# Routing early, and two experts begun on the rows of the first six sequences

## The chip, the cores and the metric

The kernel runs on one core of a Trainium2 chip. A time is the device time of one execution, in microseconds (us). The engines are called by these names: PE (TensorE, matmuls), DVE (VectorE), ACT (ScalarE), POOL (GpSimd, which also issues transfers) and SP (SyncE, which only issues transfers).

## The reference

Two stages are computed, one after the other.

```python
# attention: 8 sequences, 8 heads, 576 positions, head size 64; causal in blocks of 64
scores = scale * q @ k.T
scores = where(pos_i // 64 >= pos_j // 64, scores, -1e9)
attn_out = softmax(scores) @ v
x = attn_out.transpose(0, 2, 1, 3).reshape(4608, 512)

# experts: a hash of the token id chooses one of 8 experts for each of the 4608 rows
expert_idx = token_ids * 2654435761 % 8
for e in range(8):
    rows = expert_idx == e
    out[rows] = maximum(x[rows] @ w1[e], 0) @ w2[e]      # w1: 512 x 1024, w2: 1024 x 512
```

The multiplier is odd and leaves 1 when divided by 8, so the expert of a token is the low three bits of its id. In the data used here the experts have between 525 and 624 tokens each, and between 402 and 471 of each expert's tokens are in the first six sequences.

## The kernel before

**Attention.** The work is cut into 32 pairs of heads, four pairs for each of eight sequences, and a loop of 34 rounds (g) goes over them as a pipeline. Round g computes the scores and exponentials of pair g (`S_chunk`, three chunks, line 289 on ACT), the product with v of pair g-2 (`PV`, lines 326 and 331), its division by the row sums (`norm`, lines 343 and 346 on DVE), and the transposes of q and k for pair g+2 (`T_pair`, lines 231 and 236). The casts of q and k to bf16 are made on DVE (line 171), with a last part on POOL (line 176), those of v on POOL (`cast_v`, lines 183 to 188), three rounds ahead. The loads of q, k and v of a sequence are issued by SP (lines 105 to 132) into the pool `ld`, which has two buffers of each, so the loads of sequence b+2 wait until the casts of sequence b have been made. A finished sequence is written as 576 rows to `x_dram` by POOL (`write_x`, lines 356 and 358).

**Routing.** While attention runs, a generator `route` works out a slot for every token: each expert owns 640 slots, that is five tiles of 128 (CAP and G), and 32 spare tiles take what overflows. It counts tokens with a scan along each partition and two small matmuls, and turns the counts into slot numbers with some twenty DVE instructions (lines 373 to 448). In rounds 2 to 8 one piece of it is run in each round. Then `place_a` and `place_b` turn the slots of one sequence into a permutation: DVE builds one-hot matrices (lines 490 and 493), POOL multiplies them with row numbers (496 and 499), PE multiplies the two (509) and DVE adds the result up (512). They run in rounds 11 to 26, in turn; `placed` in round 27 writes the permutation `perm3`.

**Experts.** For every expert, `gather_x` fetches five tiles of rows of x by an indirect transfer from POOL (line 633) into ten fixed buffers, `transpose_x` transposes them on PE (645) and copies them out on DVE (646), `stage_a` multiplies with w1 (64 matmuls of 320 columns, line 657) and applies the relu on ACT (662), and `stage_b` multiplies with w2 (40 matmuls of 512 columns, line 672), copies out on DVE (677) and scatters the rows to the output from POOL (679). The order on PE is: first layer of expert e, transposes of expert e+1, second layer of expert e-1. The weights have two buffers each and are loaded by POOL (531 and 536).

The order of instructions on each engine is that in which the program writes them (`manual_schedule`). Buffers of pools that follow one another in time lie over each other: those of the expert stage take the room of the attention pools, `fix` first, then `ld`. A pool's tile waits for the readers of what lay there before.

What joins the two stages is the following. Each gather of expert 0 names the whole of `x_dram` as its source:

```python
out=xgs[g % (2 * G)][:], out_offset=None, in_=x_dram[:, :],
in_offset=bass.IndirectOffsetOnAxis(ap=perm3[:, g : g + 1], axis=0),
```

so it waits for the rows of all eight sequences.

Of the kernel before, what the change touches and what calls it, by code (L numbers as in the profile page):

```python
# [22 lines left out]
N = B * S  # L23
NT = 4
NP = H // 2
CAP = 640
G = CAP // 128
OVT = 32
NG = E * G + OVT
NEG = -30000.0  # L30
# [4 lines left out]
def kernel(  # L35
# [50 lines left out]
    psS = att_ctx.enter_context(tc.tile_pool(name="psS", bufs=2, space=bass.MemoryType.PSUM))  # L86
    psT = att_ctx.enter_context(tc.tile_pool(name="psT", bufs=2, space=bass.MemoryType.PSUM))
    psO = att_ctx.enter_context(tc.tile_pool(name="psO", bufs=1, space=bass.MemoryType.PSUM))
    fix = att_ctx.enter_context(tc.tile_pool(name="fix", bufs=1))
    ld = att_ctx.enter_context(tc.tile_pool(name="ld", bufs=2))  # L90
    att = att_ctx.enter_context(tc.tile_pool(name="att", bufs=2))
    rt = att_ctx.enter_context(tc.tile_pool(name="rt", bufs=1))

# [276 lines left out]
    def route():  # L370
# [8 lines left out]
        for i in range(5):  # L379
# [19 lines left out]
        ohf = oh[:].rearrange("p e t -> p (e t)")  # L399
        nc.vector.tensor_tensor_scan(cum[:].rearrange("p e t -> p (e t)"), ohf, ohf, 0.0,  # L400
                                     op0=ALU.add, op1=ALU.bypass)
        offs = rt.tile([P, E], F32, name="offs")
        nc.vector.memset(offs[:, 0:1], 0.0)
        nc.vector.tensor_copy(offs[:, 1:E], cum[:, 0 : E - 1, T - 1])
        cnt = rt.tile([P, E], BF16, name="cnt")
        nc.vector.tensor_tensor(out=cnt[:], in0=cum[:, :, T - 1], in1=offs[:], op=ALU.subtract)
        pb = psT.tile([P, 5, 65], F32, name="pb", tag="tp")
        nc.tensor.matmul(pb[:, 0, 0:E], lhsT=lower[:], rhs=cnt[:], start=True, stop=True)
        nc.tensor.matmul(pb[:, 1, 0:E], lhsT=onesbf[:], rhs=cnt[:], start=True, stop=True)
        base = rt.tile([P, 2, E], F32, name="base")  # L410
        nc.vector.tensor_copy(base[:], pb[:, 0:2, 0:E])
        yield

        ovc = rt.tile([P, E], I32, name="ovc")
        nc.vector.tensor_scalar(ovc[:], base[:, 1, :], float(127 - CAP), 0.0, op0=ALU.add, op1=ALU.max)
        nc.vector.tensor_single_scalar(ovc[:], ovc[:], 7, op=ALU.arith_shift_right)
        ovf = rt.tile([P, E], F32, name="ovf")
        nc.vector.tensor_copy(ovf[:], ovc[:])
        inc = rt.tile([P, E], F32, name="inc")
        nc.vector.tensor_tensor_scan(inc[:], ovf[:], ovf[:], 0.0, op0=ALU.add, op1=ALU.bypass)  # L420
        e640 = rt.tile([P, E], F32, name="e640")
        nc.vector.tensor_single_scalar(e640[:], iota_e[:], float(CAP), op=ALU.mult)

        off1 = rt.tile([P, E], F32, name="off1")
        nc.vector.tensor_tensor(out=off1[:], in0=base[:, 0, :], in1=offs[:], op=ALU.subtract)
        off2 = rt.tile([P, E], F32, name="off2")
        nc.vector.tensor_tensor(out=off2[:], in0=inc[:], in1=ovf[:], op=ALU.subtract)
        nc.vector.tensor_scalar(off2[:], off2[:], 128.0, float(E * CAP - CAP), op0=ALU.mult, op1=ALU.add)
        nc.vector.tensor_tensor(out=off2[:], in0=off2[:], in1=e640[:], op=ALU.subtract)
        nc.vector.tensor_tensor(out=cum[:], in0=cum[:], in1=off1[:, :, None].to_broadcast([P, E, T]), op=ALU.add)  # L430
        ovm = rt.tile([P, E, T], F32, name="ovm")
        nc.vector.tensor_single_scalar(ovm[:], cum[:], float(CAP) + 0.5, op=ALU.is_gt)
        nc.vector.tensor_tensor(out=ovm[:], in0=ovm[:], in1=off2[:, :, None].to_broadcast([P, E, T]), op=ALU.mult)
        nc.vector.tensor_tensor(out=cum[:], in0=cum[:], in1=ovm[:], op=ALU.add)
        nc.vector.tensor_tensor(out=cum[:], in0=cum[:], in1=e640[:, :, None].to_broadcast([P, E, T]), op=ALU.add)
        nc.vector.scalar_tensor_tensor(out=cum[:], in0=cum[:], scalar=-1.0, in1=oh[:],
                                       op0=ALU.add, op1=ALU.mult)
        yield
        slf = rt.tile([P, T], F32, name="slf")
        nc.vector.tensor_reduce(slf[:], cum[:].rearrange("p e t -> p t e"), axis=AX.X, op=ALU.add)  # L440
# [93 lines left out]
    def load_w2(e):  # L534
        w2b = wts.tile([P, FF // P, DM], BF16, name="w2b", tag="w2b")
        nc.gpsimd.dma_start(w2b[:], moe_w2[e].rearrange("(p fb) o -> p fb o", p=P))
        w2s[e] = w2b


    NPAIRS = B * NP  # L540
    both = (nc.sync, nc.scalar)
    load_qk(0, 0, 2, rest=False, engs=both)
    load_qk(0, main=False, engs=both)
    load_qk(0, 2, 8, rest=False, engs=both)
    load_v(0)
    nc.sync.dma_start(tid[:], moe_token_ids.rearrange("(b s) -> b s", b=B))
    load_qk(1)
    load_v(1)
    rgen = route()
# [3 lines left out]
    for w in range(2):  # L553
        cast_qk(0, w, 0, 0)
    T_rest(0)
    for w in range(2):
        cast_qk(0, w, 1, 2, rest=False)

    steps = {g: (lambda: next(rgen, None)) for g in range(2, 9)}
    steps[7] = rows  # L560
    for j in range(B):
        steps[11 + 2 * j] = lambda j=j: place_a(j)
        steps[12 + 2 * j] = lambda j=j: place_b(j)
    steps[27] = placed
    for g in range(NPAIRS + 2):
        b, pr = divmod(g, NP)
        live = g < NPAIRS
        nxt = live and b + 1 < B
        if live:
            S_chunk(g, 0)  # L570
        if g >= 2:
            PV(g - 2, 0)
        if live:
            S_chunk(g, 1)
        if g >= 2:
            PV(g - 2, 1)
            norm(g - 2)
        if live:
            S_chunk(g, 2)
            if pr == 0:  # L580
                S_rest(b)
        if g == 0:
            T_pair(1)
        if g < 2:
            for w in range(2):
                cast_qk(0, w, g + 2, g + 3, rest=False)
        if g + 2 < NPAIRS:
            T_pair(g + 2)
        for gv in range(NP) if g == 0 else (g + 3,):
            bv, pv = divmod(gv, NP)  # L590
            if bv < B:
                cast_v(bv, pv)
                if pv == 0:
                    cast_v4(bv)
        if g in steps:
            steps[g]()
        if nxt:
            if pr == 0:
                cast_qk(b + 1, 0, 0, 2)
            elif pr == 1:  # L600
                cast_qk(b + 1, 1, 0, 2)
            elif pr == 2:
                T_rest(b + 1)
                cast_qk(b + 1, 0, 2, 4, rest=False)
            else:
                cast_qk(b + 1, 1, 2, 4, rest=False)
        if pr == 1 and b >= 1:
            write_x(b - 1)
        if pr == (1 if b == 0 else 0) and b + 2 < B:
            load_qk(b + 2)  # L610
            load_v(b + 2)
        if 6 <= g < 6 + 2 * G:
            nc.gpsimd.memset(xgs[g - 6][:], 0.0)
        if pr == 0 and b == 6:
            load_w1(0)
        if pr == 0 and b == 7:
            load_w2(0)
    att_ctx.close()


# [6 lines left out]
    HC = CAP // 2  # L627
    xtiles = {}

    def gather_x(e):  # L630
        for t in range(G):
            g = e * G + t
            nc.gpsimd.indirect_dma_start(  # L633
                out=xgs[g % (2 * G)][:], out_offset=None, in_=x_dram[:, :],
                in_offset=bass.IndirectOffsetOnAxis(ap=perm3[:, g : g + 1], axis=0),
                bounds_check=N - 1, oob_is_err=False,
            )

    def transpose_x(e):
        xT = mx.tile([P, NKT, CAP], BF16, name="xT", tag="xT")  # L640
        for t in range(G):
            xg = xgs[(e * G + t) % (2 * G)]
            tp = psX.tile([P, NKT, P], BF16, name="tpx", tag="tpx")
            for db in range(NKT):
                nc.tensor.transpose(out=tp[:, db, :], in_=xg[:, db * P : (db + 1) * P], identity=identbf[:])  # L645
            nc.vector.tensor_copy(xT[:, :, t * P : (t + 1) * P], tp[:])  # L646
        xtiles[e] = xT

    def stage_a(e):
        w1b = w1s[e]  # L650
        xT = xtiles[e]
        hT = mx.tile([P, NFT, CAP], BF16, name="hT", tag="hT")
        for ft in range(NFT):
            hp = psH.tile([P, 2, 512], F32, name="hp", tag="hp")
            for db in range(NKT):
                for t in range(2):
                    nc.tensor.matmul(  # L657
                        hp[:, t, 0:HC], lhsT=w1b[:, db, ft::NFT],
                        rhs=xT[:, db, t * HC : (t + 1) * HC],
                        start=(db == 0), stop=(db == NKT - 1),  # L660
                    )
            nc.scalar.activation(hT[:, ft, :].rearrange("p (t n) -> p t n", t=2), hp[:, :, 0:HC], ACT.Relu)  # L662
        return hT

    out_writes = []

    def stage_b(e, hT):
        w2b = w2s[e]
        for tt in range(G):
            yp = psY.tile([P, DM], F32, name="yp", tag="yp")  # L670
            for ft in range(NFT):
# [14 lines left out]
                tc.declare_no_dep(ins.ins, w.ins, reason="rows of different tokens")  # L686
            out_writes.append(ins)

    gather_x(0)
    gather_x(1)  # L690
    load_w1(1)
    load_w2(1)
    hts = {}
    transpose_x(0)
    for e in range(E):
        hts[e] = stage_a(e)
        if e + 2 < E:
            load_w1(e + 2)
        if e + 1 < E:
            transpose_x(e + 1)  # L700
        if e + 2 < E:
            gather_x(e + 2)
        if e >= 1:
            stage_b(e - 1, hts.pop(e - 1))
            if e + 1 < E:
                load_w2(e + 1)
    stage_b(E - 1, hts.pop(E - 1))


    n_ov = nc.values_load(ov_i[0:1, 0:1], min_val=0, max_val=OVT)  # L710
# [68 lines left out]
```

The softmax here doesn't subtract the row's maximum and nothing guards it: scores larger than these inputs give would overflow.

## Time and profile before

| quantity | value |
|---|---|
| time, median of 3 runs (lowest to highest) | 345.86 us (343.06 to 347.33) |
| span of the profiled run | 343.6 us |
| PE, DVE, ACT, POOL busy | 277.1, 158.8, 142.8, 198.1 us |
| mean granted clock of PE | 0.926 |
| last norm of attention ends | 162.45 us |
| first matmul with w1 begins | 179.87 us |
| second layer of expert 0 begins | 204.67 us |

The page of the profile gives the busy time of each engine, then 40 slices of the span in which a digit is the busy share in tenths; PEclk is the clock that PE was granted, and the DMA line is the share of the core's 16 DMA engines. The timeline lists an engine's instructions in order, with start, duration, engine, line, operation, result and operands, count, and in brackets the idle time before it and what ended that. The list of waits gives engine and line, whom it waited for, the sum in us, how often and the longest.

### The profile page before, as it was taken

The numbers are of one execution on the slowest core, as the hardware profiler recorded it, in microseconds if no ns is written. First come the engines' busy times: TensorE is split into PE (matmuls) and PEld (weight loads), VectorE is DVE, ScalarE is ACT, GpSimd is POOL, SyncE is SP. The second block draws the span as 40 slices with busy tenths as digits, with TensorE's granted clock in tenths as the row PEclk, the third lists the DMA queues.
The fourth block names the chain that finished last, engine by engine and source line by source line (L and its number), as shares of the span: only waits on it lengthen the run. The fifth ranks groups of instructions, "written<-read, shape, count | busy, mean of one in ns | idle before, by whom it ended". The sixth has DMA issues, their size and how long they took to land. (4 is left out here: it accounts for less than half of the span.)

```text
span 343.6 us, 7894 instructions
## 1 busy us (share of the span) xinstructions
PE 277.1 (81%) x3247; PEld 201.2 (59%) x3247; DVE 158.8 (46%) x346; ACT 142.8 (42%) x169; POOL 198.1 (58%) x281
## 2 busy tenths in 40 slices
PE   1574784998878888895039989999999999999991
PEld 1342663776656666664028865949586685949540
DVE  4345769888868788863020224040413324040330
ACT  1342762887657577783004440604133140604100
POOL 3065378388988789960374647274664737232352
PEclk9997886999989899997558999999999999999998
DMA  7999997899898984672226987796969697825432
GB/s 200 284 272 283 246 273 173 216 280 268 211 288 184 285 184 78 138 134 72 69 85 126 215 194 240 167 215 176 200 203 186 231 175 225 194 77 134 129 130 75
DMA packets 67045, 64.58 MB, mean 188 GB/s; under 512 B 19378, under 2 KB 60340, under 8 KB 64960
## 3 DMA queue, kind: packets, MB, share of 16 engines
q0 software_dynamic: 12288, 35.71, 43.5%
q1 hardware_dynamic: 52064, 27.17, 32.4%
q10 hardware_dynamic: 2656, 1.18, 1.3%
q8 instruction: 26, 0.43, 0.5%
q14 instruction: 11, 0.09, 0.1%
HBM read 67.15 MB, written 15.20 MB: 240 GB/s over the span
## 5 line engine op out<-in xcount | busy, mean ns | idle before, releaser
L289 ACT ACTIVATE pt<-ps 128x1024 bf16<-128x1024 f32 x96 | 94.3, 1022 | 54.3 <-PE ps L265 54.0
L662 ACT ACTIVATE hT<-hp 128x640 bf16<-128x640 f32 x64 | 45.0, 703 | 117.1 <-PE hp L657 117.1
L657 PE MATMUL hp<-xT,w1b 128*128 128x320 bf16 x512 | 72.7, 303 | 0.6 <-DVE xT L646 0.6
L657 PEld LDWEIGHTS <-w1b 128*128 128x128 bf16 x512 | 69.9, 144 | 3.2 <-issue 1.1
L672 PE MATMUL yp<-w2b,hT 128*128 128x512 bf16 x320 | 70.2, 379 | 0.0
L679 POOL DMA_INDIRECT out_dram<-ysb,perm x40 | 39.7, 992 | 35.6 <-DVE ysb L677 26.8
L646 DVE COPY xT<-tpx 128x512 bf16<-128x512 bf16 x40 | 15.7, 422 | 79.4 <-PE tpx L645 77.4
L672 PEld LDWEIGHTS <-hT 128*128 128x128 bf16 x320 | 31.0, 98 | 36.2
L677 DVE COPY ysb<-yp 128x512 f32<-128x512 f32 x40 | 27.7, 692 | 51.7 <-PE yp L672 51.7
L633 POOL DMA_INDIRECT xg<-x_dram,perm x40 | 40.6, 1015 | 16.5 <-issue 11.9
L326 PE MATMUL O<-vx,pt 128*128 128x65 bf16 x896 | 43.7, 206 | 2.6 <-DVE xs L346 2.2
L243 PE MATMUL ps<-qkT 64*128 64x64 bf16 (+2 forms) x384 | 37.9, 280 | 2.6 <-ACT pt L289 2.2
L326 PEld LDWEIGHTS <-pt 128*128 128x128 bf16 x896 | 35.8, 105 | 6.4 <-issue 1.8
L183 POOL CAST vx<-vf 128x512 bf16<-128x512 f32 x32 | 21.1, 669 | 20.9 <-DMA vf<-in_v_dram 19.9
L645 PE MATMUL tpx<-identbf,xg 128*128 128x128 bf16 x160 | 15.0, 229 | 19.9 <-DMA xg<-x_dram,perm 16.7
L356 POOL DMA_DIRECT2D x_dram<-xs x32 | 23.3, 734 | 13.1 <-DVE xs L346 12.6
L346 DVE TENSOR_TENSOR xs<-O,rs 128x320 bf16<-128x320 f32 x64 | 28.4, 486 | 1.1
L265 PE MATMUL ps<-maskq,maskk 64*128 64x64 bf16 (+1 forms) x256 | 28.3, 214 | 0.0
L645 PEld LDWEIGHTS <-xg 128*128 128x128 bf16 x160 | 11.0, 101 | 23.7 <-DMA xg<-x_dram,perm 18.0
L236 DVE COPY qkT<-tp 128x1024 bf16<-128x1024 bf16 x32 | 22.0, 688 | 5.0 <-PE tp L231 4.0
L531 POOL DMA_DIRECT2D w1b<-in_moe_w_dram x8 | 4.9, 614 | 30.8 <-PE tpx L645 26.7
L231 PE MATMUL tp<-identbf,qb 128*128 128x128 bf16 x128 | 13.7, 233 | 8.2 <-DVE qb L171 8.0
(112 smaller groups left out, 264.3 us busy)
## 6 DMA issues: line engine op xcount, KB each, us to landing
vf<-in_v_dram SPq DMA_DIRECT2D x16, 512.0 KB, 7.1
w1b<-in_moe_w_dram POOLq DMA_DIRECT2D x8, 1024.0 KB, 8.1
w2b<-in_moe_w_dram POOLq DMA_DIRECT2D x8, 1024.0 KB, 8.6
qf<-in_q_dram SPq DMA_DIRECT2D x7, 1024.0 KB, 7.9
kf<-in_k_dram SPq DMA_DIRECT2D x14, 512.0 KB, 7.1
x_dram<-xs POOLq DMA_DIRECT2D x32, 128.0 KB, 5.8
qf<-in_q_dram SPq DMA_DIRECT2D x16, 64.0 KB, 6.7
vf<-in_v_dram SPq DMA_DIRECT2D x16, 64.0 KB, 5.8
```

Of the source, the lines that this page charges most:

```text
L243: nc.tensor.matmul(ps[:, m, o0 : o0 + n], lhsT=qk[rows, pr, 1, 128 * kt : 128 * kt + 128], rhs=qk[rows, pr, 0, q0 : q0 + n], start=first, ...
L265: nc.tensor.matmul(ps[:, m, o0 : o0 + 128 * n].rearrange("p (t h j) -> p t h j", h=2, j=16)[:, :, 0, :], lhsT=maskk[rows, c, :], rhs=maskq ...
L289: nc.scalar.activation(ptv[:, :, 512 * ch : 512 * ch + 512], ps[:], ACT.Exp, scale=SCALE)
L326: nc.tensor.matmul(O[:, t, :], lhsT=pt[:, m * PTW + o0 : m * PTW + o0 + 128], rhs=vx[:, h, i, :], start=(n == 0), stop=(n == t),)
L346: nc.vector.tensor_tensor(out=xs[:, :, 0:DM].rearrange("p t (d h k) -> p h t d k", d=4, h=H)[:, h], in0=O[:, m, :, 0:D].rearrange("p t (k ...
L633: nc.gpsimd.indirect_dma_start(out=xgs[g % (2 * G)][:], out_offset=None, in_=x_dram[:, :], in_offset=bass.IndirectOffsetOnAxis(ap=perm3[:, ...
L645: nc.tensor.transpose(out=tp[:, db, :], in_=xg[:, db * P : (db + 1) * P], identity=identbf[:])
L657: nc.tensor.matmul(hp[:, t, 0:HC], lhsT=w1b[:, db, ft::NFT], rhs=xT[:, db, t * HC : (t + 1) * HC], start=(db == 0), stop=(db == NKT - 1),)
L662: nc.scalar.activation(hT[:, ft, :].rearrange("p (t n) -> p t n", t=2), hp[:, :, 0:HC], ACT.Relu)
L672: nc.tensor.matmul(yp[:], lhsT=hT[:, ft, tt * P : (tt + 1) * P], rhs=w2b[:, ft, :], start=(ft == 0), stop=(ft == NFT - 1),)
L677: nc.vector.tensor_copy(ysb[:], yp[:])
L679: ins = nc.gpsimd.indirect_dma_start(out=out[:, :], out_offset=bass.IndirectOffsetOnAxis(ap=perm3[:, gg : gg + 1], axis=0), in_=ysb[:], in ...
```

## The change

The slots of each expert are dealt out so that its first 384, three tiles of the five, hold tokens of the first six sequences alone. (If an expert had fewer than 384 of them, the slots left over would stay empty.) Tokens of the last two sequences, and what is above 384, come after. A gather of these three tiles then needs only the rows of the first six sequences and names only those as its source. The permutation has to be known sooner for that, so that all of the routing is moved forward:

- the token ids are loaded third on ACT's queue, and not on SP's after v of sequence 0;
- the pieces of `route` run in rounds 0 to 3, `place_a` in rounds 5 to 19, `place_b` three rounds after its `place_a` (8 to 22), `placed` in round 23;
- the count is made twice for each expert, up to the end of sequence 5 and to the end; some instructions for the second count come in, and two passes over the slot array are joined into one;
- the casts of q and k come ahead of the routing steps in a round, and the cast of v after them;
- w1 of expert 0 and 1 are loaded in rounds 22 and 26, w2 of both in 24 and 30;
- three tiles of expert 0 are gathered at the end of round 27, three of expert 1 at the end of round 28;
- the pool `ld` is laid out ahead of `fix`, so that the tiles of the expert stage lie over load buffers;
- the first layer of experts 0 and 1 is made in two parts, with three tiles and with two (`stage_a_part`: 32 matmuls of 384 columns, then 32 of 256; two blocks of the hidden size share a PSUM tile and a relu). The order on PE is then: three tiles of expert 0, three of expert 1, the other two of expert 0, the other two of expert 1, second layer of expert 0, transposes and first layer of expert 2, and on as before.

```diff
+BA = 6
+EARLY = 384
+GA = EARLY // 128
...
+    ld = att_ctx.enter_context(tc.tile_pool(name="ld", bufs=2))
     fix = att_ctx.enter_context(tc.tile_pool(name="fix", bufs=1))
-    ld = att_ctx.enter_context(tc.tile_pool(name="ld", bufs=2))
...
+        na = rt.tile([P, E], F32, name="na")
+        nc.vector.tensor_single_scalar(na[:], base[:, 1, :, 0], float(EARLY), op=ALU.max)
+        tot = rt.tile([P, E], F32, name="tot")
+        nc.vector.tensor_tensor(out=tot[:], in0=na[:], in1=base[:, 1, :, 1], op=ALU.add)
...
+        nc.vector.tensor_tensor(out=off1[:, :, 1], in0=off1[:, :, 1], in1=na[:], op=ALU.add)
...
-        nc.vector.tensor_single_scalar(ovm[:], cum[:], float(CAP) + 0.5, op=ALU.is_gt)
-        nc.vector.tensor_tensor(out=ovm[:], in0=ovm[:], in1=off2[:, :, None].to_broadcast([P, E, T]), op=ALU.mult)
+        nc.vector.scalar_tensor_tensor(
+            out=ovm[:], in0=cum[:], scalar=float(CAP) + 0.5,
+            in1=off2[:, :, None].to_broadcast([P, E, T]), op0=ALU.is_gt, op1=ALU.mult)
...
+    def gather_x(e, t0=0, t1=G):
+        n = N if t1 > GA else BA * S
+        for t in range(t0, t1):
+            g = e * G + t
+            nc.gpsimd.indirect_dma_start(
+                out=xgs[g % (2 * G)][:], out_offset=None, in_=x_dram[0:n, :],
+                in_offset=bass.IndirectOffsetOnAxis(ap=perm3[:, g : g + 1], axis=0),
+                bounds_check=n - 1, oob_is_err=False,
+            )
...
     load_qk(0, 0, 2, rest=False, engs=both)
+    nc.scalar.dma_start(tid[:], moe_token_ids.rearrange("(b s) -> b s", b=B))
...
-    nc.sync.dma_start(tid[:], moe_token_ids.rearrange("(b s) -> b s", b=B))
...
-    steps = {g: (lambda: next(rgen, None)) for g in range(2, 9)}
-    steps[7] = rows
+    steps = {g: [] for g in range(NPAIRS + 2)}
+    steps[1].append(lambda: next(rgen))
+    steps[2].append(lambda: next(rgen))
+    steps[3] += [lambda: next(rgen, None), rows]
     for j in range(B):
-        steps[11 + 2 * j] = lambda j=j: place_a(j)
-        steps[12 + 2 * j] = lambda j=j: place_b(j)
-    steps[27] = placed
+        steps[5 + 2 * j].append(lambda j=j: place_a(j))
+        steps[8 + 2 * j].append(lambda j=j: place_b(j))
+    steps[23].append(placed)
...
         if g == 0:
+            next(rgen)
+            for w in range(2):
+                cast_qk(0, w, 1, 2, rest=False)
             T_pair(1)
+            next(rgen)
...
+        if g == 0:
+            next(rgen)
...
+        for step in steps[g]:
+            step()
+        bv, pv = divmod(g + 3, NP)
+        if 0 < bv < B:
+            cast_v(bv, pv)
...
-        if pr == 0 and b == 6:
-            load_w1(0)
-        if pr == 0 and b == 7:
-            load_w2(0)
+        if g in (22, 26):
+            load_w1((g - 22) // 4)
+        if g in (24, 30):
+            load_w2((g - 24) // 6)
+        if g in (27, 28):
+            gather_x(g - 27, 0, GA)
...
-    gather_x(0)
-    gather_x(1)
-    load_w1(1)
-    load_w2(1)
-    hts = {}
-    transpose_x(0)
-    for e in range(E):
-        hts[e] = stage_a(e)
+    gather_x(0, GA, G)
+    gather_x(1, GA, G)
+    for e in range(2):
+        transpose_x(e, 0, GA)
+        stage_a_part(e, 0, GA)
+    transpose_x(0, GA, G)
+    gather_x(2)
+    stage_a_part(0, GA, G)
+    load_w1(2)
+    transpose_x(1, GA, G)
+    gather_x(3)
+    stage_a_part(1, GA, G)
+    load_w1(3)
+    stage_b(0)
+    load_w2(2)
+    transpose_x(2)
+    for e in range(2, E):
+        stage_a(e)
```

## The prediction, made before the result was known

> **What bounds the kernel now.** I read the 40 slices first, because the shares of the whole span average two stages with different limits: attention (to about 162 us) and the experts (from about 175 us).
>
> ```profile
> PE   1574784998878888895039989999999999999991
> POOL 3065378388988789960374647274664737232352
> PEclk9997886999989899997558999999999999999998
> DMA  7999997899898984672226987796969697825432
> ```
>
> One slice is 8.6 us. The DMA engines are full to slice 14 (about 129 us) apart from slices 6 and 7; TensorE is full from slice 22 to the end; between the two, slices 18 to 20, nothing is full. So attention is paced by its loads, the experts by TensorE, and there is a hole. Cut into stretches (PE, PEld, DVE, ACT and POOL busy, clock, DMA share, GB/s):
>
> ```profile
> 140.00:150.00 10.00, 9.49 (x201) 7.18 (x201) 7.51 (x18) 7.77 (x9) 7.84 (x13) 1.00 0.46 91
> 160.00:170.00 10.00, 1.27 (x24) 1.11 (x21) 1.11 (x3) 0.00 (x0) 3.35 (x5) 0.50 0.24 60
> 170.00:180.00 10.00, 2.79 (x21) 1.99 (x22) 1.59 (x4) 0.00 (x0) 6.90 (x7) 0.50 0.25 69
> 200.00:220.00 20.00, 18.88 (x124) 13.50 (x123) 5.43 (x10) 5.33 (x8) 11.20 (x12) 1.00 0.80 203
> ```
>
> The timelines of POOL and TensorE around the hole say what it is made of:
>
> ```profile
> 166.06 0.56 POOL L358 DMA_DIRECT2D x_dram<-xs  x1
> 171.27 1.12 POOL L633 DMA_INDIRECT xg<-x_dram,perm  x1 [4.64 <-DMA x_dram<-xs]
> 172.69 1.03 POOL L633 DMA_INDIRECT xg<-x_dram,perm  x1 [0.30 <-issue]
> ```
> ```profile
> 161.03 0.24 PE L331 MATMUL O<-v,pt 128*128 128x65 bf16 x1
> 174.22 0.61 PE L645 MATMUL tpx<-identbf,xg 128*128 128x128 bf16 x4 [12.95 <-DMA xg<-x_dram,perm]
> 180.59 10.00 PE L657 MATMUL hp<-xT,w1b 128*128 128x320 bf16 x63 [0.25 <-DVE xT L646]
> 193.13 8.72 PE L657 MATMUL hp<-xT,w1b 128*128 128x320 bf16 x63 [0.37 <-DVE xT L646]
> ```
>
> Last attention matmul 161.3, last norm 162.45, last x row issued 166.6 and landed 171.27, first gathered tile usable 174.22, first expert matmul 180: about 19 us in which TensorE only transposes. The chain of waits is of no use here, it ends after two steps. Last, who held the loads and the place matmuls up:
>
> ```profile
> SPq L105 <- DVE qb L171: 10.1, 4, 6.7
> SPq L111 <- DVE kb L171: 5.4, 4, 2.2
> PE pq L509 <- POOL ohg L499: 8.0, 8, 1.7
> ```
>
> The 6.7 us is the q load of sequence 4 (issued 61.03): its buffer waits for a cast that VectorE does late, because at 48.6 to 55.4 it runs the long routing step. The DMA share at 58 to 62 us is 0.11.
>
> **What the Trainium skill says.** "TensorE: Matmul & The Clock Gate", part 1: the clock is half until about 3.4 us of sustained matmuls. The trace agrees: granted 0.50 from 159 to 183.1 us, and the first expert takes 10.00 us for what the second does in 8.72. Same page, "Architectural detail": GpSimd's queue is strict FIFO, so a gather that waits holds everything behind it; line 633 shows such a wait of 4.64 us. "DMA: Bandwidth & Descriptors", "SWDGE vs HWDGE vs iDMA": only one software queue context is allocated, so weight loads, x writes and gathers from POOL share one set of rings. The trace has them all in q0 but no case of an x write right behind a weight load.
>
> **The change, part by part.**
>
> *Expert start (removes the hole).* Before, from the last norm (call it E, 162.45) to the end of the first layer of expert 1 (193.13 + 8.72 = 201.85) it is 39.4 us. After, the same work can start at E, because three tiles of experts 0 and 1 hold only tokens of sequences 0 to 5 and were gathered in rounds 27 and 28, and w1 of both is loaded. A matmul costs 8.72/64 = 136 ns for 320 columns, 0.426 ns a column. Sum after E: start 0.3; transposes: five tiles took 190.42 to 193.13, and from its rows three take 1.8 and two 1.4, so 2x1.8 + 2x1.4 = 6.4; first layer 2 x 32 matmuls of 384 columns at 164 ns = 10.5, 2 x 32 of 256 columns at 109 ns = 7.0; half clock 2.0 (before it lost 10.00 - 8.72 = 1.3; one 3.4 us window at half is 1.7, and the first transposes are slow too). Total 26.2, so 13.2 saved. Unknown: the strided weight load is 144 ns long in the trace. At 320 columns it hides under 136 ns steps, so it must overlap its neighbour; at 256 columns it may not. Bounds: 109 ns, or 144 ns, which adds 64 x 35 = 2.2 us. I take 109, since PV matmuls with loads of 98 ns go by at 15 in under 0.7 us. Relu work is the same bytes and ends inside the matmuls. Moving the ld pool first lets the experts' tiles lie over buffers whose last reader is a cast of round 28, not over pt and vx, which the last PV reads: no cost, no wait.
>
> *Late rows (a new wait).* The gathers of rounds 27 and 28 wait on POOL for the x rows of sequence 5. In the rounds' spacing of the trace (about 3 us each at the end) those writes are issued until about E - 17 and land 5.8 later, E - 11. Then six gathers of 1.3 (1.0 + 0.3) and a cast: to about E - 3. Queued behind them: cast of v for the last pair (needed at E - 2, done near E - 6: free), x of sequence 6 (5 issues, 3.4 us), w2 of expert 1 (0.6), x of sequence 7 (3.4). So the last x is issued by about E + 4.5 to 6 instead of E + 4.2, behind a 1 MB weight load that takes 8.6 to land: rows in DRAM at E + 10 to 12 (before: E + 8.8), fourth tile usable 3 us on and fifth 1.3 later, E + 14 to 16.3. TensorE asks for the fourth at 0.3 + 2x1.8 + 10.5 + 2.0 = E + 16.4. So mostly hidden; VectorE is busy beside the gathers and their issue may be slower (the w1 issue took 0.84 there against 0.54 to 0.63 later; x1.5 gives +4 us). I charge 1 us, range 0 to 4. Everything after (w1 and x of expert 2 before TensorE has done layer two of expert 0, 8.8 us) stays hidden, as in the steady part, 97% busy.
>
> *Early routing.* About 16 us of VectorE move from rounds 2 to 8 to rounds 0 to 3. The first piece (3.1 us, then 0.5) falls into VectorE's own waits for q and k (4.05 us until 14.2): free if the token ids, now third on ACT's queue, are there by 9 us. The scan piece (about 2.9) delays round 1 by some 2 us, and the long step (6.8 before, about 6.3 with one fused pass) delays round 2; by round 5 I find it level with the trace (norm of pair 3 at about 46), and by round 6, without the long step, 5.5 ahead (norm of pair 4 at 50.5, not 55.99). So the 6.7 us wait of the q load goes and the DMA hole of slice 6 with it: +5. Casting k's rest ahead of v stops POOL's wait for v from holding TensorE (2.0 at 33.2); part of the same 5. Placing now lies in rounds 5 to 22: rounds 6 to 10 get slower, -1.5. The smaller waits of the loads (DMA share 0.67 and 0.63 in 90 to 94 and 106 to 110, worth 2.8) are partly cured by placing three rounds ahead of its matmuls: +1. Together 4.5, range 0 to 7.
>
> *Rounds 23 to 27.* With placing they take 4.1 us (norms at 126.53 and 142.93, four rounds); without, 3.05 (146.84 to 152.89). They keep the casts, so I take 3.3: 4 x 0.8 + a little for perm, 3.5. Range 1 to 5. The loads of w1 (0) and (1) and w2 (0) now come in rounds 22 to 26, where the DMA share was 0.67 (120 to 140 us) and falling: nothing.
>
> Sum: 13.2 - 1 + 4.5 + 3.5 = 20.2; 345.9 - 20.2 = 325.7.
>
> **The rivals.**
> 1. *Attention stays paced by its loads.* 27 MB in q1 at 250 to 280 GB/s can't go faster; what is saved in round 6 comes back as waits later. For: DMA share about 1.0 to 120 us. Against: the 0.11 stretch is real idle time. Gain 12.2 + 1.5: 332.
> 2. *The late rows become the wait.* POOL is late by the gathers, the last x stands behind w2, and TensorE waits 6 to 8 us before the fourth tile, perhaps with the clock back at half. For: one ring, FIFO. Against: TensorE has 16 us of other work first. 345.9 - 13.2 - 8 + 7: 332; with rival 1 as well, 338.
> 3. *Everything works, and the rounds run at 3.05 and DMA without holes.* 13.2 + 6 + 7.5: 319.
> 4. *Slower.* The routing on VectorE's in-order queue lies wholly open at the start (16 us), the loads never catch up (two buffers), and the gathers add a wait of some 4 at the end: 345.9 + 16 + 4 - 12 = 354. Against: VectorE is busy 7.6 and 12.1 of the first two 20 us.
>
> **How the numbers follow.** Main forecast 0.55; rival 1 0.18; rival 2 0.14 (with 1: 0.02 of it); rival 3 0.1; rival 4 0.03. Faster by 2% means under 338.9: all but rival 4 and the double case, about 0.93; within 2%, 0.04. The range takes in rivals 1 to 3: 317 to 335; rival 2 joined to rival 1, and rival 4, are outside.
>
> **What would show it.** Right: first expert matmul 2 to 3 us after the last norm; first-layer matmuls in groups of 32; x gathers on POOL before the last x writes; no SP wait over 3 us for a q load; DMA slice 6 full; place matmuls without a POOL wait. Wrong: a wait of TensorE for xg between the first and second part of expert 0; a v cast stuck behind a gather with PV waiting; a wait on token ids before 15 us; 256-column matmuls at 144 ns.

## The result, and the profile after

The changed kernel takes 324.7 us (median of four executions, 324.27 to 327.45) where the kernel before takes 346.25 beside it: ratio 0.941, 95% interval 0.934 to 0.948. On two other chips, where the kernel before took 366.4 and 359.5, the ratio was 0.952 (0.940 to 0.964) and 0.954 (0.949 to 0.958). The experiments ran on three chips (1, 2, 5 and 7 on the first, where the kernel before takes 345.85; 3, 4, 9 and 10 on the second; 6, 8, 11 and 12 on the third), so they are compared by the ratio to the kernel before on the same chip. Since the ratio of one and the same kernel differs between chips by up to 0.012, runs of different chips can be set beside each other only to about that.

The same lines of the 40 slices, of the changed kernel (a slice is now 8.1 us):

```profile
PE   1429499979798999985858989999999999999991
POOL 2083606999999999849337760764737467041362
PEclk9999699979999999996986999999999999999997
DMA  6999999989599999983933899869798696728132
```

Slices are counted from 0. DMA slices 5 to 7 are full now, with one new hole in slice 10 (81 to 89 us). The hole of PE (5, 0 and 3 in slices 18 to 20) is gone, but slices 18 and 20 show 5, and the clock drops in 18, 20 and 21. Two stretches around the join, which lies some 13 us sooner now (PE, PEld, DVE, ACT and POOL busy, clock, DMA share, GB/s):

```profile
150.00:160.00 10.00, 8.44 (x53) 6.21 (x51) 2.32 (x6) 3.24 (x4) 6.17 (x10) 0.81 0.78 143
160.00:170.00 10.00, 6.08 (x40) 4.92 (x38) 0.42 (x1) 3.24 (x4) 3.48 (x4) 0.88 0.38 104
```

POOL's timeline at the join, then PE's:

```profile
140.58 1.10 POOL L561 DMA_INDIRECT xg<-x_dram,perm  x1 [4.83 <-DMA x_dram<-xs]
...
148.75 2.88 POOL L359 DMA_DIRECT2D x_dram<-xs  x4
...
152.17 0.61 POOL L554 DMA_DIRECT2D w2b<-in_moe_w_dram  x1
152.78 2.83 POOL L359 DMA_DIRECT2D x_dram<-xs  x4
155.60 0.57 POOL L361 DMA_DIRECT2D x_dram<-xs  x1
165.61 1.09 POOL L561 DMA_INDIRECT xg<-x_dram,perm  x1 [9.44 <-DMA x_dram<-xs]
```
```profile
149.25 1.74 PE L676 MATMUL tpx<-identbf,xg 128*128 128x128 bf16 x12 [1.33 <-DVE xs L349]
151.50 6.51 PE L708 MATMUL hp<-xT,w1b 128*128 128x384 bf16 x32 [0.52 <-DVE xT L677]
...
159.74 5.40 PE L708 MATMUL hp<-xT,w1b 128*128 128x384 bf16 x32 [0.61 <-DVE xT L677]
168.52 0.61 PE L676 MATMUL tpx<-identbf,xg 128*128 128x128 bf16 x4 [3.38 <-DMA xg<-x_dram,perm]
169.66 0.61 PE L676 MATMUL tpx<-identbf,xg 128*128 128x128 bf16 x4 [0.53 <-DMA xg<-x_dram,perm]
170.79 5.40 PE L708 MATMUL hp<-xT,w1b 128*128 128x256 bf16 x32 [0.52 <-DVE xT L677]
...
177.26 3.71 PE L708 MATMUL hp<-xT,w1b 128*128 128x256 bf16 x32 [0.63 <-DVE xT L677]
```

The last norm ends at 149.1 (before 162.45), and the first matmul with w1 starts 2.4 us after it. The wait that the change was to remove has gone from the first tile; a smaller one stands at the fourth: the last x writes are issued by 156.2 and land at 165.6, 9.4 us later, where it was 4.65 before. That costs 3.38 + 0.53 us of waiting, and the clock falls: the 256-column matmuls of expert 0 take 5.40 us, those of expert 1 3.71. Of SP's waits for load buffers, 6.7 us long before, the longest left and the only one of a q or k load are:

```profile
SPq L130 <- DMA kf<-in_k_dram: 1.9, 1, 1.9
SPq L108 <- DVE kb L174: 0.4, 1, 0.4
```

So this one execution gained 13.4 us in attention. From the last norm to the end of the first layer of expert 1 (177.26 + 3.71 = 180.97) it takes 31.9 us instead of 39.4, so that the experts gained 7.5. This stretch is called the expert start below. The forecast had 8 and 12.2. The experiments ask which is right for more than this execution, and where each part comes from.

### The profile page after: what moved, and what is told of

The parts are those of the page before. It is cut to its first block, busy times and chain, and to the rows that moved or that the text cites. A ratio compares the mean times of both kernels' runs of the same rounds, so it can differ in the third digit from the quotient of the medians.

```text
span 322.5 us, 7913 instructions
## 1 busy us (share of the span) xinstructions
PE 272.9 (85%) x3247; PEld 197.8 (61%) x3247; DVE 156.6 (49%) x351; ACT 142.6 (44%) x169; POOL 196.5 (61%) x281
## 5 line engine op out<-in xcount | busy, mean ns | idle before, releaser
L694 ACT ACTIVATE hT<-hp 128x640 bf16<-128x640 f32 x48 | 33.7, 703 | 83.4 <-PE hp L689 83.4
L561 POOL DMA_INDIRECT xg<-x_dram,perm x40 | 40.6, 1015 | 25.7 <-DMA x_dram<-xs 14.3
L689 PE MATMUL hp<-xT,w1b 128*128 128x320 bf16 x384 | 53.3, 299 | 0.4 <-DVE xT L677 0.4
L329 PE MATMUL O<-vx,pt 128*128 128x65 bf16 x896 | 41.3, 199 | 7.9 <-DVE xs L349 6.6
L329 PEld LDWEIGHTS <-pt 128*128 128x128 bf16 x896 | 33.4, 101 | 11.6 <-DVE xs L349 4.8
L246 PE MATMUL ps<-qkT 64*128 64x64 bf16 (+2 forms) x384 | 36.4, 270 | 2.8 <-ACT pt L292 2.4
L186 POOL CAST vx<-vf 128x512 bf16<-128x512 f32 x32 | 23.4, 733 | 10.3 <-DMA vf<-in_v_dram 9.8
L708 PE MATMUL hp<-xT,w1b 128*128 128x384 bf16 (+1 forms) x128 | 21.0, 330 | 2.3 <-DVE xT L677 2.3
L712 ACT ACTIVATE hT<-hp 128x768 bf16<-128x768 f32 (+1 forms) x16 | 11.3, 704 | 25.8 <-PE hp L708 25.8
```

Of the source, the lines that this page charges most:

```text
L246: nc.tensor.matmul(ps[:, m, o0 : o0 + n], lhsT=qk[rows, pr, 1, 128 * kt : 128 * kt + 128], rhs=qk[rows, pr, 0, q0 : q0 + n], start=first, ...
L329: nc.tensor.matmul(O[:, t, :], lhsT=pt[:, m * PTW + o0 : m * PTW + o0 + 128], rhs=vx[:, h, i, :], start=(n == 0), stop=(n == t),)
L561: nc.gpsimd.indirect_dma_start(out=xgs[g % (2 * G)][:], out_offset=None, in_=x_dram[0:n, :], in_offset=bass.IndirectOffsetOnAxis(ap=perm3[ ...
L689: nc.tensor.matmul(hp[:, t, 0:HC], lhsT=w1b[:, db, ft::NFT], rhs=xT[:, db, t * HC : (t + 1) * HC], start=(db == 0), stop=(db == NKT - 1),)
L708: nc.tensor.matmul(hp[:, ft - f0, 0 : P * (t1 - t0)], lhsT=w1b[:, db, ft::NFT], rhs=xT[:, db, c], start=(db == 0), stop=(db == NKT - 1),)
```

## The experiments

**1. Early routing without early experts.**

```diff
-        if g in (27, 28):
-            gather_x(g - 27, 0, GA)
...
+    gather_x(0)
+    gather_x(1)
+    load_w1(1)
+    load_w2(1)
+    transpose_x(0)
+    for e in range(E):
         stage_a(e)
```

> The changed kernel's early routing and attention loop, but no early gather: the gathers, the loads of w1 and w2 of expert 1 and the order of the expert stage are those of the kernel before. Theory 1: attention alone gained 13.4 us (last norm at 149.1 instead of 162.45), and it does not depend on the early gathers, so the last norm ends at 148 to 150 and the time is about 346.2 - 13.4 = 333 (332 to 334.5). The early experts are then worth 8 us. Theory 2: the forecast's shares, attention 8 and experts 12: time about 338.

Measured: 336.8 us, ratio 0.974 (0.967 to 0.980). Attention is worth 9.1 us (2.0 to 3.3%), so the early experts are worth the rest, 336.8 - 324.7 = 12.1. The expert start takes 39.4 us in its trace, as before the change. Theory 1 falls, and with it the reading of one trace: here the last norm ended at 154.4, not 149.1. The two executions run alike to pair 8 (norms at 65.1 and 65.8); pair 10 is at 74.8 in one and 79.1 in the other, with the same instructions. Between them PE stands before the matmuls of a placing step, which in the first trace begin without a wait:

```profile
69.96 0.87 PE L527 MATMUL pq<-ohg,ohp 128*128 128x144 bf16 x5 [1.83 <-DVE qb L174]
```

After it the granted clock is 0.50 from 70 to 76 us, where it is 0.84 in the first trace. Experiment 2's trace has the same (2.11 us, clock 0.50, pair 10 at 79.6). In the first trace these matmuls begin before that cast of q, so the cast cannot be what they need; why PE stands here is open.

**2. w2 of expert 1 behind the last gathers.**

```diff
-        if g in (24, 30):
-            load_w2((g - 24) // 6)
+        if g == 24:
+            load_w2(0)
...
     gather_x(1, GA, G)
+    load_w2(1)
```

> The changed kernel with one move: the load of w2 of expert 1 is issued after the gathers of tiles 3 and 4, not ahead of the x writes of the last sequence. Theory 1: in the changed kernel TensorE waits 3.4 us for the fourth tile, its clock falls to half after that (1.7 us) and the fifth tile comes 0.5 to 0.9 late, all because the last x rows stand behind that 1 MB load (landing 9.4 us after their last issue, where it was 4.65 before). Then the last rows land about 4.7 us sooner, the wait for the fourth tile is gone or under 0.5 us, the clock stays up, and the time falls from 324.7 to 319 or 320. Theory 2: the last rows are late because POOL issues the x rows of both sequences 6 and 7 only after the gathers, and the two batches of writes hold each other up. Then landing stays 8 us or more after the last issue and the time stays within 1 us of 324.7.

Measured: 321.7 us, ratio 0.930 (0.925 to 0.936), 3 us less than the changed kernel beside an equal kernel before; the interval overlaps that of the changed kernel slightly, so the size is uncertain. In its trace (an execution of 325.3 us, with a late attention stage) POOL's wait is short again and PE's fourth tile is there:

```profile
159.44 0.56 POOL L361 DMA_DIRECT2D x_dram<-xs  x1
164.42 1.08 POOL L561 DMA_INDIRECT xg<-x_dram,perm  x1 [4.42 <-DMA x_dram<-xs]
```
```profile
167.13 5.39 PE L708 MATMUL hp<-xT,w1b 128*128 128x384 bf16 x32 [0.61 <-DVE xT L677]
172.36 0.61 PE L676 MATMUL tpx<-identbf,xg 128*128 128x128 bf16 x8
173.59 3.71 PE L708 MATMUL hp<-xT,w1b 128*128 128x256 bf16 x32 [0.63 <-DVE xT L677]
...
178.38 3.71 PE L708 MATMUL hp<-xT,w1b 128*128 128x256 bf16 x32 [0.63 <-DVE xT L677]
```

From the last norm (156.4) to 178.38 + 3.71 = 182.1 it is 25.7 us. Theory 1 holds for the mechanism. Theory 2, that the two batches of x rows hold each other up, falls by the next run, on another chip, which has w2 in place: there POOL pauses as long between the two batches (1.48 us and the 0.61 of w2, here 2.21 us), and the last rows still take 9.38 us. The gain is about 3 and not 5; a likely reason is that PE's wait is not in every execution.

**3. The changed kernel again, on the second chip.**

> The changed kernel once more, as the measure for the three runs beside it. Two of the earlier runs have the same attention loop up to round 24, and their last norms lie 5 to 7 us later than in the first profile of the changed kernel. Theory 1: attention paced by its loads differs from execution to execution by some 5 us, and in the expert stage the wait for the fourth tile takes up the difference (shorter where attention ends later): last norm anywhere from 148 to 156, time 324 to 327. Theory 2: the two were out of line for other reasons: last norm again at 148 to 150, first-layer work after it again 32 us.

Measured: ratio 0.952 (0.940 to 0.964), 349.3 us. The last norm ended at 156.9, and the wait for x was again 9.38 us, but PE waited only 0.28 for the fifth tile. For attention ended 7.8 us later than in the first trace, and POOL's gathers only 3 us later: the last rows landed at 170.0, 13.1 us after the last norm and not 16.5. So theory 1 holds for the wait. Its times do not fit this chip, and the expert start is 32.1 us again, as theory 2 said, though for another reason: PE stands 1.45 us within the matmuls of 256 columns and 3.08 us before the last 32 of them, while DVE, ACT and POOL stand for part of that time too. Such stops are in every trace of this chip (see the last section).

When is the landing long? In five traces w2 was issued at most 2.1 us before the last x writes began: the first one, this one and experiments 5, 7 and 9. The rows landed 9.44, 9.38, 9.61, 10.16 and 8.19 us after their last issue. In two traces (experiment 4 and the third run of the changed kernel) POOL waited 7 to 8 us between the issue of w2 and the last x writes, and these landed 4.70 and 4.83 us after their issue. So the distance from w2 decides, and not an early end of attention (in experiment 7 the last norm ends at 165.1). That late rows take back what attention gains would explain why times scatter by 3 us while last norms scatter by more; with one trace for each run it is not shown.

**4. The casts of v ahead of the others, as before.**

```diff
+        bv, pv = divmod(g + 3, NP)
+        if 0 < bv < B:
+            cast_v(bv, pv)
+            if pv == 0:
+                cast_v4(bv)
         if nxt:
...
         for step in steps[g]:
             step()
-        bv, pv = divmod(g + 3, NP)
-        if 0 < bv < B:
-            cast_v(bv, pv)
-            if pv == 0:
-                cast_v4(bv)
```

> The changed kernel with the casts of v ahead of the casts of q and k and of the routing steps in a round, as before. Theory 1: GpSimd then waits for v of the next sequence before it casts the rest of k, TensorE's transposes of that rest wait with it, as at 33 us in the kernel before (2 us), and again for each sequence whose loads are late: time 326 to 330. Theory 2: the order on GpSimd does not matter where the loads set the pace: within 1 us of the changed kernel.

Measured: 348.8 us, ratio 0.958 (0.949 to 0.966), beside 349.3 for the changed kernel. Theory 2, as far as these runs can tell: the intervals leave room for some 5 us either way.

**5. Routing pieces back in rounds 2 to 8.**

```diff
-    steps[1].append(lambda: next(rgen))
-    steps[2].append(lambda: next(rgen))
-    steps[3] += [lambda: next(rgen, None), rows]
+    for r in (2, 3, 4, 5, 6, 8):
+        steps[r].append(lambda: next(rgen, None))
+    steps[7].append(rows)
...
-        steps[5 + 2 * j].append(lambda j=j: place_a(j))
-        steps[8 + 2 * j].append(lambda j=j: place_b(j))
-    steps[23].append(placed)
+        steps[8 + 2 * j].append(lambda j=j: place_a(j))
+        steps[11 + 2 * j].append(lambda j=j: place_b(j))
+    steps[26].append(placed)
...
         if g == 0:
-            next(rgen)
             for w in range(2):
```

> The changed kernel with the routing pieces back in rounds 2 to 8, placing in rounds 8 to 25, still three rounds apart, the permutation in round 26, and the early gathers in 27 and 28 as in the change. Theory 1: the long routing step in round 5 makes the cast late and opens the 4 us hole in the loads again (the norm of pair 4 goes from 50.8 back to about 55), which the loads never catch up: time 329 to 331. Theory 2: what matters is only that no placing lies beside the last rounds and that placing does not hold TensorE up; the moved pieces are paid in rounds 0 to 3 just as well: time 324 to 326.5.

Measured: 334.5 us, ratio 0.967 (0.961 to 0.973), 9.8 us more than the change. The norm of pair 4 is at 56.9 and SP's wait for a q buffer is back:

```profile
SPq L108 <- DVE qb L174: 7.4, 2, 6.9
```

Theory 1, and by more than it said: the 345.9 - 334.5 = 11.4 us that are left are about what the early experts alone gave by experiment 1 (12.1), so most of attention's 9 us is gone. In the one trace some is left: the last norm ends at 160.1, 2.4 us sooner than before, and the expert start takes 32.6 us, with a wait of 2.48 and 0.67 us for late rows. The placing had to move by three rounds with the pieces; experiment 6 asks what that is worth.

**6. Placing in late rounds.** Experiment 1 with placing at 11 + 2j, its matmuls at 14 + 2j, `placed` in round 29.

```diff
-        steps[5 + 2 * j].append(lambda j=j: place_a(j))
-        steps[8 + 2 * j].append(lambda j=j: place_b(j))
-    steps[23].append(placed)
+        steps[11 + 2 * j].append(lambda j=j: place_a(j))
+        steps[14 + 2 * j].append(lambda j=j: place_b(j))
+    steps[29].append(placed)
```

> The kernel of the run experts_after (early routing pieces and the new order of casts, gathers and experts as before), with placing moved back to late rounds: one-hot matrices in rounds 11 to 25, their matmuls three rounds after (14 to 28), permutation in round 29. Theory 1: taking placing out of the last rounds is worth 3.5 us as forecast, so those come back: 340 to 341 where experts_after took 336.8 beside a kernel before of 345.85 (ratio 0.983 to 0.987 instead of 0.974). Theory 2: only the distance of three rounds matters, not where placing lies: within 1.5 us of experts_after (ratio 0.97 to 0.978).

Measured: 350.3 us, ratio 0.973 (0.968 to 0.978), as experiment 1 (0.974). Theory 1 falls: placing in early rounds gives no 3.5 us. That it is worth nothing at all (theory 2) is less sure, since the two runs are of different chips and the changed kernel's own ratio is 0.012 higher on this one; late placing may even be the better. The norms show what early placing costs in the first rounds: pair 10 is at 70.7 here, at 77.3 and 74.6 in the two traces of this chip with early placing (experiments 12 and 11). What it brings in the last rounds they do not show: pairs 20 to 28 take 31.3 us here and 27.6 in experiment 1, but 34.3 and 30.6 in those two traces of this chip, which have no placing there either.

**7. The placing matmuls one round after their one-hot matrices.**

```diff
-        steps[8 + 2 * j].append(lambda j=j: place_b(j))
+        steps[6 + 2 * j].append(lambda j=j: place_b(j))
```

> The changed kernel with the placing matmuls one round after their one-hot matrices, as before, instead of three. Theory 1: the distance of three rounds is worth most of what rounds 12 to 22 gained beyond the forecast (about 5 us), because TensorE no longer waits about 1 us for GpSimd in each of eight rounds: time 327 to 330, and the waits of the place matmuls for POOL come back at 6 to 8 us in total. Theory 2: in these rounds the loads set the pace and hide such waits: the waits come back, but the time stays within 1.5 us of 324.7.

Measured: 335.4 us, ratio 0.971 (0.967 to 0.976), 10.7 us more. Its waits:

```profile
PE pq L527 <- POOL ohg L517: 14.7, 7, 3.3
```
```profile
64.71 0.66 PE L527 MATMUL pq<-ohg,ohp 128*128 128x144 bf16 x5 [3.29 <-POOL ohg L517]
```
```profile
SPq L108 <- DVE acc L530: 13.0, 4, 4.2
SPq L114 <- DVE kb L174: 8.4, 5, 2.3
```

Theory 1, at twice its size. PE's wait is up to 3.3 us and not 1.7 as in the kernel before. In the four long ones (3.29, 3.26, 3.25 and 2.24 us) POOL comes late to the one-hot matrices because it first issues the x rows of a sequence (3.4 to 4.1 us), casts v and, in three of them, clears gather buffers; it waits for no load there. DVE waits in turn to add the product, and the casts behind it hold the loads.

**8. The kernel before, with this distance of three rounds.**

```diff
...
-        steps[12 + 2 * j] = lambda j=j: place_b(j)
-    steps[27] = placed
+        steps[14 + 2 * j].append(lambda j=j: place_b(j))
+    steps[29].append(placed)
```

> The kernel before with one thing of the change: the placing matmuls three rounds after their one-hot matrices (rounds 14 to 28), permutation in round 29. Theory 1: TensorE loses its eight waits for GpSimd, 8.0 us in total in the kernel before, of which the loads hide half or more: faster by 2 to 4 us (ratio 0.988 to 0.994). Theory 2: this distance alone carries most of the 9 us that attention gained: ratio 0.973 to 0.98. Theory 3: in the kernel before placing stands ahead of the casts, so nothing but those short waits depends on the distance, and the loads hide them all: ratio 0.995 to 1.003.

Measured: 357.2 us beside 359.5, ratio 0.993 (0.989 to 0.996): 2.3 us by the medians, 2.7 by the ratio, theory 1. In the old order the distance is worth little; in the new one it is worth 10.7 us (experiment 7).

**9. The fixed buffers laid out ahead of the load buffers, as before.**

```diff
+    fix = att_ctx.enter_context(tc.tile_pool(name="fix", bufs=1))
     ld = att_ctx.enter_context(tc.tile_pool(name="ld", bufs=2))
-    fix = att_ctx.enter_context(tc.tile_pool(name="fix", bufs=1))
```

> The changed kernel with the pool of the load buffers laid out after the fixed buffers, as before, so that the experts' tiles lie over v, exponentials and x rows. Theory 1 (the forecast): no cost, since the first transposes stand behind the last PV on TensorE anyway: within 1 us of the changed kernel. Theory 2: the tiles then wait for readers that end later, such as the write of the last x rows out of xs, whose room they take: the first transpose's copy waits until those have landed, 9 to 16 us after the last norm, and the time rises to 332 to 340.

Measured: 354.6 us beside 349.3, ratio 0.965 (0.954 to 0.976) against 0.952. The medians are 5.4 us apart, the intervals overlap, and the trace shows the wait, first on DVE, then on PE:

```profile
168.45 0.75 DVE L677 COPY xT<-tpx 128x512 bf16<-128x512 bf16 x2 [11.58 <-DMA x_dram<-xs]
```
```profile
157.01 1.01 PE L676 MATMUL tpx<-identbf,xg 128*128 128x128 bf16 x8 [1.33 <-DVE xs L349]
168.92 0.58 PE L676 MATMUL tpx<-identbf,xg 128*128 128x128 bf16 x4 [10.90 <-DVE xT L677]
```

Theory 2: the new tiles lie over the x buffers, whose last reader is the write of the last x rows. Both last norms end at 156.9, and the expert start takes 39.4 us here and 32.1 in experiment 3: 7.3 more and not 11. For experiment 3 has some 4 us of stops in it (1.45, and 3.08 where 0.63 is usual), and this trace one of 1.38. How much of the wait reaches the time is therefore uncertain.

**10 and 11. The early gathers behind the x rows of sequence 6.** Experiment 2, and

```diff
-        if g in (27, 28):
-            gather_x(g - 27, 0, GA)
+        if g in (29, 30):
+            gather_x(g - 29, 0, GA)
```

> The changed kernel with w2 of expert 1 loaded behind the last gathers and the two early gathers moved to the ends of rounds 29 and 30, behind the x writes of sequence 6. Theory 1: GpSimd no longer waits 4 to 5 us for the rows of sequence 5 and writes the rows of sequence 6 at once, so the last rows, alone in the rings, land about 4.7 us after their issue, and nothing of the expert start is waited for: last norm to end of the first layer of expert 1 26 us, time 317 to 321. Theory 2: the gathers now end too late, since they start only with round 29: TensorE waits for the first tiles by 2 to 4 us after the last norm, and the time is that of the variant with w2 late, 321.7, or longer.

Measured: 343.3 us beside 349.3 for the changed kernel, ratio 0.939 (0.926 to 0.952) against 0.952. POOL's waits:

```profile
140.89 2.82 POOL L359 DMA_DIRECT2D x_dram<-xs  x4 [1.95 <-DVE xs L349]
...
144.57 1.12 POOL L561 DMA_INDIRECT xg<-x_dram,perm  x1 [0.30 <-issue]
...
164.33 1.08 POOL L561 DMA_INDIRECT xg<-x_dram,perm  x1 [4.90 <-DMA x_dram<-xs]
```

The gather finds its rows landed, and the last rows land in 4.90 us. PE waits for no gathered tile: from the last norm (155.7) to the end of the first layer of expert 1 (183.3) it is 27.6 us, of which PE stands 0.9 us with no reason that the profile shows. The second comparison, on a third chip and with more rounds:

> The version that was fastest so far (early gathers behind the x rows of sequence 6, w2 of expert 1 behind the last gathers), beside the changed kernel on one chip and with more rounds. Theory 1: it takes away all waits of the expert start, 5 to 6 us: ratio to the kernel before lower by 0.014 to 0.018 than that of the changed kernel, 318 to 320 us where that takes 324.7. Theory 2: the 6 us of the first comparison are chance, and moving w2 alone gives what there is: 321 to 323.

Measured: 341.2 us beside 343.4 for the changed kernel. Its six executions lie between 332.7 and 342.4, too far apart for a ratio. So it is 6 us once and 2 once. That these waits go is shown by both traces (in the second the rows land in 5.08 us, and the expert start takes 26.4); how much of it reaches the time is not settled.

**12. The changed kernel beside it.**

> The changed kernel as the measure for the runs beside it. Theory 1: on a chip on which the kernel before takes about 346 us it takes 323.5 to 327 again, ratio 0.935 to 0.945. Theory 2: the ratio is that of the second chip, 0.952, whatever the time of the kernel before.

Measured: 343.4 us, ratio 0.954 (0.949 to 0.958). Theory 2: on the chips where both kernels are slower the gain is 16 to 17 us, not 21.5. There the last rounds of attention are longer: from the norm of pair 26 to that of pair 31 it is 21.5 us here and 19.9 in experiment 3, against 14.9 in the first trace. The kernel before does not seem to lose this time, for with the one edit of experiment 8 it takes 15.1 us on the third chip; the 5.0 and 6.6 us are of the size of what is missing from the gain (4.3 and 5.5). The early gathers alone are not the cause, since experiment 6, which has none, takes 18.5.

## Why the prediction was right

The time is right (325.7 forecast, 324.7 measured), and so are its two halves: attention 8 forecast, 9.1 by experiment 1; experts 12.2 forecast, 12.1 by the same difference. The mechanism of the experts is the forecast's. That the sum for attention came out is in good part luck, since one of its two terms was about half of what it should be and the other brought nothing. The signs that were named for being right all appeared; of those for being wrong one did, PE's wait for xg between the two parts of expert 0.

- **Expert start, 13.2 saved.** Right. The sum of 26.2 us from last norm to end of the first layer is 25.7 in experiment 2, where nothing is waited for. 384 columns: 5.40 us for 32 matmuls; 256 columns: 3.71, or 116 ns each, near the lower bound of 109, so the strided weight load of 144 ns stays hidden. The half clock cost 6.51 - 5.40 = 1.1 us here and 1.0 to 2.5 in the other traces (first parts of 6.42 to 7.91 us), so that 2.0 was fair. The Trainium skill ("TensorE: Matmul & The Clock Gate", part 1) says that the clock falls to half after an idle window of about 3.4 us and stays there until about as long a stretch of work. The second drop agrees: after the wait of 3.38 us the clock was 0.59 and 0.50 from 167 to 173 us, and 1.00 again from 176. The first, 0.67 and 0.50 from 146 to 152 us, came with no single wait over 1.33 us in these 6, though PE was busy for only 3.5 of them.
- **Layout of `ld`, "no cost, no wait".** The move is free, but its reason was wrong. I named v and the exponentials as what the tiles would otherwise lie over; it is the x buffers that count, and without the move a wait of 10.9 us stands in the place of the one removed (experiment 9).
- **Late rows, 1 us (0 to 4).** The mechanism is the forecast's, with the size missed in the shown execution: 3.9 of waiting and 5.40 - 3.71 = 1.7 of half clock. The term that failed is the landing. I let w2 and the x rows land together at "E + 10 to 12"; they landed at 165.6, E + 16.5. One or two microseconds of this are the issue, done at E + 7.1 and not E + 4.5 to 6, because the six gathers moved the write of sequence 6 to E - 0.3. The rest is the landing itself, 9.4 us after that. The Trainium skill ("DMA: Bandwidth & Descriptors", "SWDGE vs HWDGE vs iDMA") says that one software context is allocated, and gives no price for standing behind another load in it; 8.2 to 10.2 us with w2 just ahead and 4.4 to 5.1 otherwise fit it. They would also fit a mere sharing of the DMA engines, whose share was 0.89 or more from 155 to 161 us; the runs do not separate the two. The effect on the time is about 3 us (experiment 2), within the range. This was rival 2 in part: the wait was real, 4 us and not 6 to 8.
- **Early routing, 4.5 = 5 - 1.5 + 1.** Its first step was right to about a microsecond: the norm of pair 0 comes 9.5 us later than before (35.95 and 26.43), that of pair 3 level at 47.2 (46 forecast, 46.7 before), that of pair 4 at 50.8 (50.5 forecast, 56.0 before), and the wait of 6.7 us is gone. Its size was too low: undone, it costs 9.8 us (experiment 5). The minus for placing in rounds 6 to 10 was too small (pair 10 comes 4 to 7 us later than with late placing, experiment 6), and so was the relief after it: pairs 10 to 20 take 37.6 us where they took 43.8.
- **Rounds 23 to 27, 3.5.** Falls as a gain of its own. Rounds without placing do take 3.3 us (norms of pairs 21 to 25, 116.7 to 130.0), but placing only moved to earlier rounds, and in sum no gain is seen (experiment 6). This term, too high, and that for early routing, too low, cancelled.
- **v behind the other casts, "part of the same 5".** Not seen (experiment 4), though an effect of the 2 us named would be too small for these runs.
- **Rival 1** (loads set the pace, gains come back) is not what happened to routing, whose gain did not come back, but it is what seems to have happened to placing.

What is open: why PE stands before the placing matmuls at 70 us in some executions and not in others, which parts them by 4 to 5 us; why the last rounds are longer on two of the chips; and how much experiments 10 and 11 gain over moving w2 alone.

## What to carry to other kernels

When a stage waits for the last piece of data, order the data so that the first work needs only early pieces; then look at what shares the queue with the last piece, for that is the new wait. Work moved out of a crowded stretch is a gain only if it lands in idle time: the routing moved to the first rounds, where the engines wait for loads, and gave most of 9 us; the placing moved between two full stretches and gave nothing that can be seen. A producer that stands behind other work on its engine needs its consumer put further off: three rounds instead of one were worth 10.7 us here.

## What the runs showed of the hardware

On the second and third chip all eight traces show stops in the expert stage. PE and ACT stop together for 0.5 to 3 us once or twice in most experts, after the first 16 or 24 matmuls of the first layer; where PE's wait is put down to ACT, ACT itself has no release that explains it. An example from the third run of the changed kernel:

```profile
221.52 2.34 PE L689 MATMUL hp<-xT,w1b 128*128 128x320 bf16 x16
224.40 1.25 PE L689 MATMUL hp<-xT,w1b 128*128 128x320 bf16 x8 [0.55 <-issue]
227.20 5.59 PE L689 MATMUL hp<-xT,w1b 128*128 128x320 bf16 x40 [1.55 <-ACT hT L694]
```

On the first chip the 64 matmuls run through in 8.72 us there, and none of its traces has such a stop from expert 2 on. The change is not the cause: the kernel before with the one edit of experiment 8 has the stops too (2.47, 1.21, 1.97, 1.90 and 1.93 us), and takes 196.8 us from its last norm to its end on the third chip, where the kernel before takes 181.2 on the first. What causes them is open.
